# A layer norm, a state-space scan and a gated feed-forward layer on one core: four equal chunks in a hand-planned order, B and C transposed by DMA

## The chip, the cores and the metric

The kernel runs on 1 core of one Trainium2 chip. The metric is the device time of one execution in microseconds (us), lower is better. A kernel is timed several times, in turns with the kernel before on the same chip. Each run carries the span of the core and the mean clock that TensorE was granted. A run counts as "slow" when it is over 1.5% above the fastest run of its kernel; only fast runs enter ratios. The profile's "span" leaves out some 2 us that the timed figure includes.

Engines are named as in the profile: PE is TensorE (matmul), DVE is VectorE, ACT is ScalarE, POOL is GpSimd, SP is SyncE, which here only issues DMAs. Each engine works through its own queue of instructions in order.

## The reference, cut to what matters

Sequence 2048, model width 448, feed-forward width 1792, all bf16.

```python
xn = layernorm(x)                                   # over 448, no scale or bias
# A: diagonal complex state-space layer, 448 states
Lam_bar = exp(dt * Lam);  B_bar = ((Lam_bar - 1) / Lam)[:, None] * B
h[t] = Lam_bar * h[t-1] + B_bar @ xn[t]             # complex, 2048 steps
s = 2 * real(C @ h) + xn * Dskip
# B: gated feed-forward
g = silu((sigmoid(xn @ w_gate) * (xn @ w_up)) @ w_down)
out = x + s * g
```

Both kernels work in chunks of tokens. For a chunk, PE multiplies the transposed normalised input (`xnT`) with gate and up weights (14 "units" `gu`, each one gate and one up tile) and with B (4 units `bu`); ACT evacuates these; DVE rotates, scans and rotates back (the complex recurrence as two real scans) and forms the gated product `hF`; PE then does the down product and the y product (skip term plus C times h) for each 128-token tile.

## The kernel before

Chunks of 256, 512, 512, 512 and 256 tokens. The statistics of the layer norm are taken on DVE, but what turns a variance into 1/sqrt(var) runs for all but the first chunk on GpSimd as Newton steps on tiny tiles. All but the first two chunks' `xn` are transposed by DMA, whose source must be padded with a 64-column copy on GpSimd.

```python
CHUNKS = [(0, 2), (2, 4), (6, 4), (10, 4), (14, 2)]     # first tile, tiles of 128 tokens
N_PE_TR = 2                                             # chunks whose x is transposed on PE

def stat_chain(g):
    G = nc.vector if g == 0 else nc.gpsimd
    ...
    for _ in range(3):                                  # Newton steps for 1/sqrt
        G.tensor_tensor(out=t, in0=y, in1=y, op=ALU.mult)
        G.tensor_tensor(out=t, in0=t, in1=ve, op=ALU.mult)
        G.tensor_scalar(out=t, in0=t, scalar1=-0.5, scalar2=1.5, op0=ALU.mult, op1=ALU.add)
        G.tensor_tensor(out=y, in0=t, in1=y, op=ALU.mult)
    ...
def norm(c, i):                                         # from the third chunk on
    nc.scalar.activation(xm[:], x_all[:, tt, :], ACT.Identity, bias=nmean[:, tt, :])
    nc.scalar.activation(xn[:, i, 0:448], xm[:], ACT.Copy, scale=rsd[:, tt, :])
    nc.gpsimd.tensor_copy(out=xn[:, i, 448:512], in_=xn[:, i, 384:448])
def b_steps():                                          # B (and likewise C): load, then transpose on PE
    ...
    for m in range(7):
        nc.tensor.transpose(tp[:, m, :], b_t[:, m, kt * P:(kt + 1) * P], ident[:, :])
def gu_unit(c, xnT, ft, half_first):
    if c == 0:                                          # tanh form, in the first chunk only
        nc.scalar.activation(th[:], gu[:, 0, 0:n], ACT.Tanh, scale=0.5)
        ...
```

## Time and profile before

Median 242.36 us (241.81 to 245.34).

| engine | busy, us | share of the 238.9 us span |
|---|---|---|
| PE | 204.5 | 86% |
| DVE | 179.4 | 75% |
| ACT | 127.4 | 53% |
| POOL | 36.3 | 15% |

These lines are from the profile's page of the kernel before. The rows with digits cut the span into 40 equal slices; a digit is the busy share of a slice in tenths, and PEclk the granted TensorE clock in tenths of full speed.

```profile
span 238.9 us, 3346 instructions
...
PE 204.5 (86%) x1146; PEld 98.1 (41%) x1160; DVE 179.4 (75%) x444; ACT 127.4 (53%) x254; POOL 36.3 (15%) x102
...
PE   7589538697974999989739999999999999999990
...
DVE  7999179998799999999995792799666369533204
...
PEclk9889955999998999999959999999999999999997
```

Shares over the whole span hide that the limit moves. Counted from 0, PE is poorly used in slices 4 to 7 and has two deep dents at 12 and 20; DVE is full in the middle; after slice 20 PE is full and DVE is not. These are the two costliest of PE's waits (columns: what waited, for what, us in total, times, longest):

```profile
PE bu L425 <- DMA xnT<-xn: 10.1, 2, 5.7
PE tpx L226 <- DVE xn L211: 8.9, 6, 4.9
```

Of DVE's waits, this one:

```profile
DVE xn L211 <- POOL rsd L201: 6.4, 1, 6.4
```

Two stretches in the windows view (stretch, its length, then busy us and instructions of PE, PE weight load, DVE, ACT and POOL, then granted clock, DMA share, GB/s):

```profile
80.00:120.00 40.00, 36.62 (x181) 15.21 (x184) 39.37 (x80) 26.67 (x48) 16.61 (x30) 1.00 0.07 16
124.00:228.50 104.50, 103.72 (x585) 50.67 (x591) 64.70 (x146) 51.32 (x106) 0.50 (x2) 0.99 0.05 16
```

PE stood still twice, 4.5 and 5.7 us, for a transposed x. DVE waited 6.4 us for `rsd` (one over the standard deviation of each token), which GpSimd makes, and PE's transposes waited for DVE in turn. The trace shows why it was late: GpSimd had begun this chain at 13.71 us, then stood 8.9 us before a copy for C whose DMA had not landed, with the rest of the chain behind that copy; it ended at 31.33. Its two later chains, with nothing foreign in them, took 10.7 and 16.2 us. Between 80 and 120 us DVE was busy 39.4 of 40 us, and after 124 us PE 103.7 of 104.5.

### The profile page before, as it was taken

The numbers are of one execution on the slowest core, as the hardware profiler recorded it, in microseconds if no ns is written. First come the engines' busy times: TensorE is split into PE (matmuls) and PEld (weight loads), VectorE is DVE, ScalarE is ACT, GpSimd is POOL, SyncE is SP. The second block draws the span as 40 slices with busy tenths as digits, with TensorE's granted clock in tenths as the row PEclk, the third lists the DMA queues.
The fourth block names the chain that finished last, engine by engine and source line by source line (L and its number), as shares of the span: only waits on it lengthen the run. The fifth ranks groups of instructions, "written<-read, shape, count | busy, mean of one in ns | idle before, by whom it ended". The sixth has DMA issues, their size and how long they took to land.

```text
span 238.9 us, 3346 instructions
## 1 busy us (share of the span) xinstructions
PE 204.5 (86%) x1146; PEld 98.1 (41%) x1160; DVE 179.4 (75%) x444; ACT 127.4 (53%) x254; POOL 36.3 (15%) x102
## 2 busy tenths in 40 slices
PE   7589538697974999989739999999999999999990
PEld 2246316343431444433314444344444455555550
DVE  7999179998799999999995792799666369533204
ACT  3468713478891736676703563874546273533232
POOL 2010720482000068830000000000000000000000
PEclk9889955999998999999959999999999999999997
DMA  6999900000211000011110000020000000000001
GB/s 133 351 277 272 348 27 0 4 0 0 44 23 25 0 19 0 0 44 22 22 41 0 25 0 19 0 65 1 19 19 3 19 0 19 22 21 21 22 0 40
DMA packets 15608, 11.75 MB, mean 49 GB/s; under 512 B 6083, under 2 KB 14662, under 8 KB 15590
## 3 DMA queue, kind: packets, MB, share of 16 engines
q1 hardware_dynamic: 15536, 11.41, 17.2%
q0 software_dynamic: 48, 0.11, 0.4%
q8 instruction: 9, 0.15, 0.3%
q14 instruction: 9, 0.07, 0.1%
q10 hardware_dynamic: 6, 0.00, 0.0%
HBM read 8.37 MB, written 1.84 MB: 43 GB/s over the span
## 4 chain that ended last, share of the span: by engine, by line
PE 48%; DVE 28%; DMA 10%; ACT 5%; POOL 3%; issue 3%; SPq 2%; DVEq 0%; POOLq 0%
PE gu L419 16%; PE acc L586 14%; PE acc L594 6%; DVE wv L517 6%; DMA wk<-in_B_w_gate_dram 5%; PE bu L419 5%; PE gu L425 3%; DMA bc<-in_A_C_im_dram 3%; DMA xnT<-xn 2%; DVE z L510 2%; DVE ta L506 2%; DVE hF L456 2%; DVE tb L508 1%; DVE hT L536 1%; DVE td L534 1%
## 5 line engine op out<-in xcount | busy, mean ns | idle before, releaser
L451 ACT ACTIVATE sig<-gu 128x512 bf16<-128x512 f32 (+1 forms) x56 | 30.4, 543 | 44.8 <-PE gu L425 34.5
L419 PE MATMUL gu<-xnT,wg 128*128 128x512 bf16 (+1 forms) x201 | 47.0, 340 | 2.9 <-ACT ub L455 1.2
L419 PE MATMUL gu<-xnT,wu 128*128 128x512 bf16 (+1 forms) x207 | 48.1, 340 | 0.2
L586 PE MATMUL acc<-wd,hF 128*128 128x448 bf16 x224 | 47.4, 357 | 0.9 <-DVE hF L456 0.8
L456 DVE TENSOR_TENSOR hF<-sig,ub 128x512 bf16<-128x512 bf16 (+1 forms) x56 | 21.0, 385 | 22.9 <-ACT ub L455 22.6
L586 PEld LDWEIGHTS <-hF 128*128 128x128 bf16 x224 | 22.3, 99 | 22.8 <-issue 2.0
L455 ACT CAST ub<-gu 128x512 bf16<-128x512 f32 (+1 forms) x56 | 29.6, 528 | 0.0
L419 PEld LDWEIGHTS <-wu 128*128 128x128 bf16 x210 | 20.8, 99 | 16.4 <-DMA wu<-in_B_w_up_dram 0.2
L419 PEld LDWEIGHTS <-wg 128*128 128x128 bf16 x210 | 17.6, 98 | 23.6 <-issue 12.9
L419 PE MATMUL bu<-xnT,bT 128*128 128x512 bf16 (+1 forms) x103 | 23.9, 367 | 0.7 <-ACT bus_606 L476 0.7
L425 PE MATMUL gu<-xnT,wk 64*128 64x512 bf16 (+1 forms) x140 | 21.2, 343 | 1.3 <-DMA wk<-in_B_w_up_dram 0.6
L594 PE MATMUL acc<-cT,hT 128*128 128x448 bf16 x98 | 20.8, 352 | 0.0
L600 ACT ACTIVATE sigd<-acc 128x448 bf16<-128x448 f32 x16 | 8.7, 544 | 16.1 <-PE acc L586 16.1
L425 PE MATMUL bu<-xnT,bT 64*128 64x512 bf16 (+1 forms) x35 | 7.1, 350 | 11.5 <-DMA xnT<-xn 10.1
L419 PEld LDWEIGHTS <-bT 128*128 128x128 bf16 x105 | 9.8, 104 | 13.0 <-issue 7.1
L594 PEld LDWEIGHTS <-hT 128*128 128x128 bf16 x112 | 11.0, 98 | 10.1
L216 POOL COPY xn<-xn 128x64 bf16<-128x64 bf16 x10 | 4.3, 426 | 70.8 <-ACT xn L215 70.8
L604 DVE TENSOR_TENSOR g_t<-zb,sigd 128x448 bf16<-128x448 bf16 x16 | 6.1, 384 | 11.4 <-ACT zb L602 11.4
L425 PEld LDWEIGHTS <-wk 64*128 64x128 bf16 x140 | 5.2, 94 | 14.3 <-issue 12.6
L226 PE MATMUL tpx<-ident,xn 128*128 128x128 bf16 x24 | 3.3, 279 | 8.9 <-DVE xn L211 8.9
L610 DVE TENSOR_TENSOR sg<-acc,g_t 128x448 bf16<-128x448 f32 x14 | 8.6, 618 | 2.6 <-PE acc L594 2.4
L170 DVE BATCH_NORM_STATS2 stats<-x_all 128x6 f32<-128x448 bf16 x16 | 9.7, 608 | 0.0
(269 smaller groups left out, 299.2 us busy)
## 6 DMA issues: line engine op xcount, KB each, us to landing
out_dram<-o_t SPq DMA_DIRECT2D x16, 112.0 KB, 1.7
wd<-in_B_w_down_dram SPq DMA_DIRECT2D x1, 1568.0 KB, 9.3
x_all<-in_A_x_dram SPq DMA_DIRECT2D x3, 448.0 KB, 7.8
wg<-in_B_w_gate_dram SPq DMA_DIRECT2D x1, 960.0 KB
wu<-in_B_w_up_dram SPq DMA_DIRECT2D x1, 960.0 KB, 11.1
wg<-in_B_w_gate_dram SPq DMA_DIRECT2D x1, 384.0 KB, 5.5
wu<-in_B_w_up_dram SPq DMA_DIRECT2D x1, 384.0 KB, 6.4
bc<-in_A_B_re_dram SPq DMA_DIRECT2D x1, 336.0 KB, 10.7
```

The costliest lines, as they stand in the source:

```text
L170: nc.vector.bn_stats(out=stats[:], in_=x_all[:, t0 + i, :])
L419: nc.tensor.matmul(banks[i][:, 0:n], lhsT=fulls[i](kt), rhs=xnT[:, kt, 0:n], start=(kt == 0 and not half_first), stop=(kt == KF - 1 and ha ...
L425: nc.tensor.matmul(banks[i][:, 0:n], lhsT=halves[i], rhs=xnT[lo:lo + H, 3, 0:n], start=half_first, stop=not half_first)
L451: sg_ins = nc.scalar.activation(sig[:, 0:n], gu[:, 0, 0:n], ACT.Sigmoid).ins
L455: nc.scalar.copy(out=ub[:, 0:n], in_=gu[:, 1, 0:n])
L456: anchors["hF"] = nc.vector.tensor_tensor(out=hF, in0=sig[:, 0:n], in1=ub[:, 0:n], op=ALU.mult).ins
L517: V.tensor_tensor_scan(out=cell["wv"][:, k, 0:n], data0=rb, data1=cell["z"][:, k, 0:n], initial=(st[pt][:, k, :] if c else 0.0), op0=ALU.m ...
L586: nc.tensor.matmul(dacc[:, 0:D], lhsT=hFs[c][:, ft, j * P:(j + 1) * P], rhs=wd[:, ft, :], start=(ft == 0), stop=(ft == FT - 1))
L594: nc.tensor.matmul(y[:, 0:D], lhsT=hTs[c][:, hm, j * P:(j + 1) * P], rhs=K["cT"][:, cm, :], start=False, stop=(i == 6))
L600: nc.scalar.activation(sigd[:], dacc[:, 0:D], ACT.Sigmoid, scale=half)
L604: nc.vector.tensor_tensor(out=g_t[:], in0=zb[:], in1=sigd[:], op=ALU.mult)
L610: nc.vector.tensor_tensor(out=sg[:], in0=y[:, 0:D], in1=g_t[:], op=ALU.mult)
```

## The change

The intent is to keep PE full throughout: equal 512-token chunks, an order of every engine's instructions laid down by a small planner with estimated durations ("late" work that is ready at a time, "side" work that fills DVE's gaps), B and C brought in already transposed by DMA so that PE and ACT are rid of 60 block transposes, and the tanh form of the gate for the larger first chunk. The diff is 1322 lines; its core, with cuts marked:

```diff
-CHUNKS = [(0, 2), (2, 4), (6, 4), (10, 4), (14, 2)]
-N_PE_TR = 2
+CT = 4                       # tiles in a chunk; NCH = 4 chunks
+N_TANH = FT + 2              # gates in the tanh form
 ...
-    nc.sync.dma_start(out=b_t[:, 0:3, 0:448], in_=A_B_re[0:384, :].rearrange("(i p) d -> p i d", p=P))
 ...
+    def load_b():
+        for k, mat in enumerate((A_B_re, A_B_im)):
+            nc.sync.dma_start_transpose(out=bT[:, 0:3, a:a + 384], in_=mat[0:384, 0:384])
+            if k == 0:
+                nc.sync.dma_start_transpose(out=bw[:], in_=mat[0:384, 320:448])
 ...
+    load_w(512, 1152)
+    load_b()
+    load_w(1152, F)
 ...
+    T_CHAIN = 9.0            # the planner's estimate of GpSimd's statistics chain
+    def stat_chain(g, t0, n):            # 19 GpSimd instructions, 26 before; 3 Newton steps as before
+        plan.add_late(plan.dve + T_CHAIN, 0.15, fin)      # fin: rsd = 1/sd_b, on DVE
 ...
+    def norm_slot(tt, on_vector):
+        xm = norm_a(tt, False)                            # ACT
+        plan.force(lambda: tt // CT in rs_done)
+        norm_b(tt, xm, False)                             # ACT, needs rsd
+        dup(tt)                                           # GpSimd: 64-column copy
+        dma_transpose(tt)
 ...
+    def b_fix():
+        nc.gpsimd.tensor_copy(out=bT[LO, 3, 0:384], in_=bw[HI, 0, :])
+    run_phase(G(0, 2, 8) + mixed(G(0, 8, 14), Bs(0), 2), [], spread(norms(1, True), 4, 5) + [(3, b_fix)])
+    ssm(0)                   # puts the scan of chunk 0, C's scaling and the statistics of chunk 3 into DVE's side list
+    ssm(1)
+    u = mixed(G(1, 0, 4), []) + mixed(G(1, 4, 8), Bs(1)) + G(1, 8, 14)
+    run_phase(u, spread(downs(0), 1, 8), spread(norms(2), 2, 8))
 ...
```

## The prediction

> **What bounds the kernel now.** The page gives PE 86%, DVE 75%, ACT 53% busy of a 238.9 us span; the limit moves. The chain of waits and the timeline show:
> - Head: the first gate/up matmul starts at 10.85 us.
> - 10.8 to 46.5 us: only the 256-token chunk 0. PE is busy 15.0 us of 10.8 to 30 and 5.2 of 30 to 40; it waits for x statistics (DVE waits 6.4 us for GpSimd), then transposes x tiles and 28 B blocks.
> - 40 to 120 us: DVE is busy 39.4 of 40 us from 80 to 120. PE stalls twice for the transposed x (4.46 and 5.66 us), and resumes at granted clock 0.62 and 0.50.
> - 124 to 228.5 us: PE-bound, 103.7 of 104.5 us busy, DVE only 64.7.
>
> **PE work that remains.** From starts in the timeline: a pair of gate/up units takes 3.23 us (153.31 to 156.54), a down tile 2.65, a y tile 1.52. My sum per 512-token chunk: 14 units 22.6 + B units 5.7 + four downs 10.6 + four y 6.1 = 45 us; four chunks 180 us. The 28 B and 32 C block transposes on PE, about 8 us with waits, go to DMA.
>
> **DVE work.** At the starts in the chain (0.60 us a 1024-wide multiply, 1.20 a scan), a chunk's scan part is 23 us; all DVE work is about 175 us, unchanged: the float32 tanh gate product now covers 16 x 512 columns. The 256-wide one took 0.42, so I estimate 0.65: +4.5 us. DVE and PE are nearly balanced, so the order must overlap them throughout.
>
> **Sum.** Statistics of four tiles precede the first norm, so the first gate/up matmul slips to about 12; two units in halves make it worth a full-rate start near 14. 14 + 180 + 4 (last product, add, store) = 198 us. Losses I add: 2 us in chunk 0, where ACT has 14 x 1.05 + sines 5.5 + B copies 4.3 = 24 us against about 25 of PE; 2 us spread (DVE has about 43 us of work against 39 of PE in the chunk-1 phase). Span 202; the wall time was 2 to 3.5 over the span before. **Predicted 205 us, 198 to 217** (8 in 10); faster by 2%: 0.97, within 0.02, slower 0.01.
>
> **DMA.** B's DRAM transposes stand before the last third of the gate/up weights on one queue. One 128x512 on-chip transpose took 1.19 us to issue, 2.4 to land. Scaled by 128x128 blocks, B's eight issues are about 10 us: weights land near 25, needed near 28. The Trainium skill, "DMA: Bandwidth & Descriptors", section "Latency and other measured facts", gives 261 GB/s for DMA transposes: 3.5 us for B's 0.92 MB, an estimate. The trace before has none from DRAM.
>
> **What would show it.** PE busy above 88%; no PE gap over 2 us after the first unit; PE-bound last three chunks; B and C transposes landing before first use; the x transposes never on PE's wait list.
>
> **What would make it wrong.** (1) DRAM transposes much slower to issue: PE waits for the last weights or bT at 28 to 35 us. (2) The GpSimd copy of the last tile of chunk 2 stands behind the statistics chain for chunk 3; a late DVE starves PE there. (3) A stall above 3 us costs more afterwards: the Trainium skill, "TensorE: Matmul & The Clock Gate", section "HAM oscillation", says idle gaps over about 3.4 us halve the clock; this trace agrees, clock 0.50 after the 5.66 us gap.

## The result, and the profile after

Median 223.56 us of four runs (220.67 to 225.65); two of the four were slow, and so was the profiled one. The ratio to the kernel before is 0.911 (95% interval 0.898 to 0.925): faster by 9%, where 205 us would have been 15%. A ratio is the mean time of one kernel's fast runs over that of the other's fast runs of the same rounds, so it is not quite the ratio of the medians quoted. Time and ratio lie above the predicted range.

The changed kernel was run again unaltered.

> The changed kernel again, unedited, as the control of this set: 220 to 222 us in its fast runs.

Measured: median 222.06 us, mean of its fast runs 221.7, ratio 0.915 (0.906 to 0.924), profile fast. It is the control below: "the changed kernel" means this profile unless said otherwise. Its page:

```profile
span 219.2 us, 2849 instructions
...
PE 195.6 (89%) x978; PEld 82.4 (38%) x978; DVE 178.0 (81%) x379; ACT 121.3 (55%) x218; POOL 34.0 (15%) x88
...
PE   7789976979993899929999999999999999959992
...
DVE  5756982946994299996589999999999999999943
...
PEclk9999999999999699966999999999999999999999
```

Against before, the second half is as planned: PE slices of 9 almost to the end. What is left of the weak stretch are three dents, in slices 6, 12 and 17, the last two with a lower clock after them. PE's waits name them:

```profile
PE bu L476 <- ACT bus L548: 5.4, 2, 4.3
PE gu L470 <- DMA xnT<-xn: 4.4, 1, 4.4
PE bu L476 <- POOL bT L831: 2.9, 1, 2.9
PE acc L678 <- DVE g_t L686: 2.3, 2, 1.2
```

Here `bu` is PE's product with B and `bus` ACT's copy of it, which frees PE's output memory for the next one; `bT` is the transposed B; `g_t` is DVE's gated output, which frees the memory of the y product (`acc`).

The three longest waits are 2.88, 4.29 and 4.43 us, 11.6 together, and have three different names behind the arrow: a GpSimd copy, an ACT copy, a DMA. The timeline of PE shows where they lie (start, length, engine, line, operation, and in brackets the idle time before it):

```profile
34.95 0.39 PE L476 MATMUL bu<-xnT,bT 64*128 64x512 bf16 x2 [2.88 <-POOL bT L831]
...
71.94 0.61 PE L476 MATMUL bu<-xnT,bT 64*128 64x512 bf16 x2 [4.29 <-ACT bus L548]
...
97.44 1.46 PE L470 MATMUL gu<-xnT,wg 128*128 128x512 bf16 x3 [4.43 <-DMA xnT<-xn]
```

Now GpSimd's timeline in the same execution, with the starts and ends of three runs of its statistics chain (19 small instructions each):

```profile
24.63 0.68 POOL L241 CAST var_b<-mv 128x4 bf16<-128x4 f32 x1 [13.47 <-DVE mv L226]
...
33.68 0.65 POOL L260 TENSOR_TENSOR sd_b<-y,ve 128x4 bf16<-128x4 f32 x1
34.40 0.50 POOL L831 COPY bT<-bw 64x384 bf16<-64x384 bf16 x1
...
58.69 0.95 POOL L241 CAST var_b<-mv 128x4 bf16<-128x4 f32 x1 [15.88 <-DVE mv L226]
...
64.30 0.99 POOL L256 TENSOR_TENSOR q<-y 128x4 f32<-128x4 f32 x1
...
66.02 0.98 POOL L258 TENSOR_SCALAR q<-q 128x4 f32<-128x4 f32 x1
...
67.72 0.20 POOL L256 TENSOR_TENSOR q<-y 128x4 f32<-128x4 f32 x1
...
68.84 0.20 POOL L260 TENSOR_TENSOR sd_b<-y,ve 128x4 bf16<-128x4 f32 x1
...
84.87 0.56 POOL L241 CAST var_b<-mv 128x4 bf16<-128x4 f32 x1 [2.69 <-DVE mv L226]
...
94.42 0.34 POOL L260 TENSOR_TENSOR sd_b<-y,ve 128x4 bf16<-128x4 f32 x1
94.71 0.23 POOL L293 COPY xn<-xn 128x64 bf16<-128x64 bf16 x1
```

- First stall: the copy that finishes B's transpose (`bT`, 34.40) stands behind the chain of chunk 1, which runs from 24.63 to 34.33. PE starts at 34.95. The copy takes 0.50 us, and its data was there long before: that transpose was issued at 12.48 and landed 4.3 us later.
- Third stall: the 64-column copy of chunk 2's last tile (94.71) stands behind the chain of chunk 3, from 84.87 to 94.76. The DMA transpose is issued at 94.97 and PE starts at 97.44.
- Second stall: the chain of chunk 2 ends at 69.04. DVE then makes `rsd`; ACT, whose queue has the norm of chunk 2 ahead of a copy that PE needs, waits for it. ACT's timeline:

```profile
69.35 0.67 ACT L289 ACTIVATE xn<-xm,rsd 128x448 bf16<-128x448 bf16 x1 [5.35 <-DVE rsd L263]
...
70.87 1.02 ACT L548 CAST bus<-bu 128x1024 bf16<-128x1024 f32 x1
```

ACT stood still 5.35 us before `xn`, although the copy `bus` behind it needed nothing from the norm. PE got its bank of memory back after 71.9.

Why does a chain of 19 instructions on 128x4 elements take 10 us? From 67.72 on, with DVE idle, its instructions take 0.20 us each. Before that they take up to 0.99. The next fence is DVE's timeline beside them:

```profile
64.09 1.22 DVE L584 TENSOR_TENSOR_SCAN wv<-r_col,z 128x512 bf16<-128x512 f32 x1
...
65.80 1.21 DVE L584 TENSOR_TENSOR_SCAN wv<-r_col,z 128x512 bf16<-128x512 f32 x1
...
69.07 0.18 DVE L263 RECIPROCAL rsd<-sd_b 128x4 f32<-128x4 bf16 x1 [1.49 <-POOL sd_b L260]
```

The GpSimd instruction that began at 64.30 ended at 65.29; the DVE scan beside it ran from 64.09 to 65.31. The one from 66.02 ended at 67.00, the scan at 67.01. GpSimd waited for DVE's instruction to end. The Trainium skill, "SBUF — State Buffer", section "Who interferes with whom", says this: a DVE instruction with two SBUF inputs and a GpSimd instruction that reads SBUF share one read interface, and the one that comes second is blocked for the whole instruction. This trace agrees. So the chain is slow because DVE is busy: at 0.28 us from start to start, as from 67.72 on, 19 instructions would take about 5.3 us (an estimate), and the other half is waiting. Experiment 3 shows the same chain in 5.6 us, started where DVE has little to do.

A word on the clock. The Trainium skill, "TensorE: Matmul & The Clock Gate", section "HAM oscillation", puts the limit of an idle gap at about 3.4 us. In this profile the gap of 2.88 us left the clock at full, those of 4.29 and 4.43 us were followed by 0.50. In the first, slow profile the same first gap was 3.58 us long and half clock followed it. Over all profiles, after the first 10 us, the limit is not so sharp. Every PE gap of 3.58 us or more was followed by half clock, and none of 1.2 to 1.46 us was; between them both happened. A gap of 2.14 us was followed by 0.50 in experiment 4 and by full clock in experiment 7, one of 3.10 us by 0.50 in experiment 9 and one of 3.16 us by full clock in experiment 8. So whether half clock follows a gap of 1.6 to 3.2 us can't be read from its length. That may be why this kernel's runs scatter; it was not tested by itself.

### The profile page after: what moved, and what is told of

The parts are those of the page before. It is cut to its first block, busy times and chain, and to the rows that moved or that the text cites. A ratio compares the mean times of both kernels' runs of the same rounds, so it can differ in the third digit from the quotient of the medians.

```text
span 223.9 us, 2849 instructions
## 1 busy us (share of the span) xinstructions
PE 199.6 (89%) x978; PEld 83.6 (37%) x978; DVE 178.2 (80%) x379; ACT 121.5 (54%) x218; POOL 33.4 (15%) x88
## 4 chain that ended last, share of the span: by engine, by line
DVE 51%; PE 22%; POOL 12%; ACT 8%; issue 4%; DMA 1%; POOLq 0%; ACTq 0%
DVE wv L584 9%; PE gu L470 8%; PE acc L665 5%; DVE stats L225 3%; DVE hT L604 3%; PE acc L680 3%; DVE g_t L686 3%; DVE tb L565 2%; DVE ta L565 2%; DVE hFa L526 2%; DVE z L578 2%; DVE hFb L526 2%; PE bu L470 2%; DVE x_all L687 2%; PE wps L214 2%
## 5 line engine op out<-in xcount | busy, mean ns | idle before, releaser
L519 ACT ACTIVATE sig<-gu 128x512 bf16<-128x512 f32 x40 | 23.9, 597 | 30.2 <-PE gu L476 22.8
L665 PE MATMUL acc<-wd,hFb 128*128 128x448 bf16 x112 | 23.8, 353 | 0.0
L665 PE MATMUL acc<-wd,hFa 128*128 128x448 bf16 x112 | 23.8, 353 | 0.0
L520 ACT CAST ub<-gu 128x512 bf16<-128x512 f32 x40 | 23.2, 581 | 0.0
L470 PE MATMUL bu<-xnT,bT 128*128 128x512 bf16 x84 | 23.1, 412 | 0.0
L515 ACT ACTIVATE th<-gu 128x512 f32<-128x512 f32 x16 | 9.5, 596 | 12.6 <-PE gu L476 9.5
L665 PEld LDWEIGHTS <-hFa 128*128 128x128 bf16 x112 | 11.0, 98 | 10.7
L665 PEld LDWEIGHTS <-hFb 128*128 128x128 bf16 x112 | 11.0, 98 | 10.2
L526 DVE TENSOR_TENSOR hFa<-sig,ub 128x512 bf16<-128x512 bf16 x19 | 7.9, 417 | 7.2 <-ACT ub L520 7.1
L686 DVE TENSOR_TENSOR g_t<-acc,g_t 128x448 bf16<-128x448 f32 x16 | 9.9, 618 | 1.9 <-PE acc L680 1.8
```

The source lines that it names most:

```text
L470: nc.tensor.matmul(banks[i][:, cols], lhsT=fulls[i](kt), rhs=xnT[:, kt, cols], start=(kt == 0 and not half_first), stop=(kt == KF - 1 and ...
L515: nc.scalar.activation(th[:], gu[:, 0, :], ACT.Tanh, scale=0.5)
L519: nc.scalar.activation(th[:], gu[:, 0, :], ACT.Sigmoid)
L520: nc.scalar.copy(out=ub[:], in_=gu[:, 1, :])
L526: V.tensor_tensor(out=hF, in0=th[:], in1=ub[:], op=ALU.mult)
L665: nc.tensor.matmul(dacc[:, 0:D], lhsT=hF_at(c, ft)[:, j * P:(j + 1) * P], rhs=wd[:, ft, :], start=(ft == 0), stop=(ft == FT - 1))
```

## The experiments

Gains are given as differences of ratios times the 242 us of the kernel before, because the runs had different chips. Theory Q: the missing 17 us are PE and DVE waiting for results that stand behind the statistics chain in GpSimd's queue. Its rivals: the DRAM transposes deliver B late; a late DVE is the real limit, so that reorders on GpSimd give almost nothing; and (T, tried last) the chain costs time by itself, whatever stands behind it. Three kinds of test tell them apart: move what stands behind the chain (1 to 4), change only its length (5 to 7), and relieve or load DVE (8 to 10).

**1. B's copy first.** The copy now stands ahead of the chain in GpSimd's queue; it ran at 16.23 us.

```diff
+    nc.gpsimd.tensor_copy(out=bT[LO, 3, 0:384], in_=bw[HI, 0, :])     # right after a dummy Silu
 ...
-    run_phase(..., spread(norms(1, True), 4, 5) + [(3, b_fix)])
+    run_phase(..., spread(norms(1, True), 4, 5))
```

> The copy of the last rows of B into bT (0.50 us on GpSimd) is put ahead of the statistics chain of chunk 1 in GpSimd's order. Theory Q (GpSimd's queue): PE's 3.58 us wait for this copy goes, the half clock after it too, and DVE's 5.88 us idle at 35 us; bw landed long before, so the copy runs near 18 us; time falls by about 6 us against the changed kernel's fast 221.4. Rival R (the DRAM transposes are late): the wait stays and is ended by a transfer into bT or bw; time within 1 us. Rival D (DVE's total work alone sets the end): the wait goes but time falls by under 2 us.

Measured 217.92 us, ratio 0.9031 (0.8977 to 0.9085). The wait for `bT` is gone from PE's list and nothing else came in its place; the other two stalls stay:

```profile
PE bu L476 <- ACT bus L548: 5.4, 2, 4.3
PE gu L470 <- DMA xnT<-xn: 4.4, 1, 4.4
```

The gain by ratios is 2.9 us, half of what was expected. The expectation was sized from the slow profile, where the gap was 3.58 us and half clock followed; in the fast control it was 2.88 with no half clock. Since PE no longer waits for `bT` at all, the data was there: the rival of late DRAM transposes falls.

**2. The 64-column copy on ACT.** It then no longer stands behind the chain of chunk 3.

```diff
-        dup(tt)
+        nc.scalar.activation(xns[tt // CT][:, tt % CT, 448:512], xm[:, 384:448], ACT.Copy, scale=rsd[:, tt, :])
```

> The 64-column copies of chunks 2 and 3 go from GpSimd to ACT, so the last one no longer stands behind the statistics chain of chunk 3. All theories: PE's 4.42 us wait for xnT at 97 to 101.7 us goes. Rival P (each PE stall costs itself and the half clock after it): time falls by about 6 us. Theory Q with DVE behind: DVE was busy through this stall but for 1.90 us, so PE only reaches the first y tile earlier and waits there for DVE; time falls by 1 to 3 us.

Measured 218.71 us, ratio 0.9044 (0.8989 to 0.9098), 2.6 us by ratios. PE's wait for the DMA of `xnT` is gone. The stall and the half clock after it were worth 4.43 and some 2.3 us; less came back, within the 1 to 3 us that theory Q expected with DVE close behind. DVE is nearly full after the stall: 87.6 of 90 us from 110 to 200 us in the control (PE 87.7). That PE then waits for DVE instead is likely but not shown by this run, whose only profile is a slow one.

**3. Chunk 2's statistics earlier.** They move ahead of the sign flips and coefficients in DVE's list, so that the chain starts sooner (at 48.85 us, as it turned out, where it was 58.69).

```diff
     side.append((0.0, emit_edges))
+    for i in range(4):
+        side.append((0.7, lambda i=i: stat(2, 8, i, 4)))
+    side.append((0.0, lambda: stat_chain(2, 8, 4)))
     side.append((0.9, emit_neg))
     side.append((2.2, emit_coeffs))
-    for i in range(4):
-        side.append((0.7, lambda i=i: stat(2, 8, i, 4)))
-    side.append((0.0, lambda: stat_chain(2, 8, 4)))
```

> The statistics of chunk 2 are taken before the sign flips and coefficients, in DVE's idle stretch at 50.6 to 55.2 us, so their GpSimd chain starts about 10 us earlier. Theory Q: ACT's 5.36 us wait for the reciprocal goes, with it PE's 4.29 us wait for bus and about 7 us of DVE idle at 72 to 80 us; time falls by about 6 us. Rival D: the order of the same DVE work changes nothing; within 2 us.

Measured 218.6 us, ratio 0.9042 (0.8983 to 0.9102), 2.7 us by ratios. The longest PE wait for ACT's `bus` fell from 4.29 to 1.1 us. Again about half of what was expected. GpSimd's chain, first and last instruction:

```profile
48.85 0.29 POOL L241 CAST var_b<-mv 128x4 bf16<-128x4 f32 x1 [5.93 <-DVE mv L226]
...
54.26 0.20 POOL L260 TENSOR_TENSOR sd_b<-y,ve 128x4 bf16<-128x4 f32 x1
```

The same 19 instructions took 5.6 us here and 10.35 in the control; DVE was busy 3.6 us of them here, mostly with instructions of 0.16 us, and 8.9 there. So part of the gain can come from the shorter chain and not from its place. ACT is now the busy one of the stretch: DVE's wait for `ctmp`, which ACT makes for C, rose from 3.8 us in one piece to 5.3 in four.

**4. All three together.**

> All three edits. Theory Q: the DVE idle that goes is about 5.9 + 7 + 1.9 = 15 us, so about 206 to 208 us, near the 205 predicted, with DVE over 90% busy from 20 us to the end and no PE wait over 2 us before the tail. Rival P: the three PE stalls with their half-clock stretches, about 19 us, go: 202 us. Rival D: 217 us or more.

Measured 210.81 us, ratio 0.8731 (0.8687 to 0.8776), 10.2 us by ratios. The three single gains sum to 8.2 us; their intervals are 1.3 to 1.5 us either way and the control's is 2.1, so whether they add is not settled. The time is 2.8 us above the 206 to 208 expected, and one PE wait over 2 us is left before the tail. PE's longest waits in this kernel:

```profile
PE acc L678 <- DVE g_t L686: 3.3, 3, 2.1
PE bu L476 <- ACT bus L548: 2.5, 2, 1.4
```

And stretches of its windows view:

```profile
100.00:140.00 40.00, 38.65 (x196) 16.32 (x194) 39.26 (x76) 25.65 (x49) 0.00 (x0) 1.00 0.09 22
140.00:180.00 40.00, 40.00 (x205) 17.48 (x204) 39.23 (x72) 19.64 (x37) 0.00 (x0) 1.00 0.04 12
181.00:183.00 2.00, 0.03 (x1) 0.03 (x1) 1.93 (x6) 0.00 (x0) 0.00 (x0) 1.00 0.00 0
183.00:187.00 4.00, 3.69 (x12) 1.40 (x12) 3.85 (x8) 0.00 (x0) 0.00 (x0) 0.57 0.08 29
```

No wait names GpSimd or a DMA any more, except GpSimd's at the start of the warm-up. PE is busy 40.0 of 40 us from 140 on, and DVE over 39 of 40 from 100 on: both are full there. At 181 us PE waits 2.14 us for DVE's `g_t`, and the clock falls to 0.57 on average over the next 4 us, 0.50 between 184 and 187.

**5 and 6. The length of the chain alone.** No reorder; only the number of Newton steps changes, 3 to 1 and 3 to 6. (One step was still accurate enough for the comparison with the reference.)

```diff
-        for _ in range(3):
+        for _ in range(1):        # and 6 in the other run
```

> One Newton step in place of three in the three GpSimd chains (8 of 19 instructions, about 4.1 us, less in each; the result moves by less than bfloat16 rounding); every order stays. Theory Q: the bT copy runs near 31.6 us, before PE needs it at 32.7; ACT's wait for the reciprocal falls from 5.4 to about 1 us; the copy of the last tile of chunk 2 comes 4 us earlier; all three PE waits shrink below 1.5 us and time falls by 8 to 11 us, close to the three reorderings together. Rival R (late transposes) and rival D (DVE's total): within 2 us, as no transfer and no DVE work changes.

> Six Newton steps in place of three: 12 more GpSimd instructions, about 6.2 us more per chain. Theory Q: all three PE waits grow by about 6 us each, to 9 to 11 us; time rises by 15 to 19 us, to about 237 to 240. Rival R and rival D: within 2 us.

Measured: one step 213.44 us, ratio 0.8795 (0.8712 to 0.8879), a gain of 8.6 us; six steps 234.81 us, ratio 0.9697 (0.9622 to 0.9772), a loss of 13.2. With one step (a slow profile) the wait for `bT` is gone and that for the DMA of `xnT` is 1.0 us, but the longest for `bus` is still 2.7, over the 1.5 expected. PE's waits with six steps:

```profile
PE bu L476 <- ACT bus L548: 8.8, 2, 7.6
PE gu L470 <- DMA xnT<-xn: 7.7, 1, 7.7
PE bu L476 <- POOL bT L831: 6.0, 1, 6.0
```

All three stalls grew by about the same amount: 2.88 to 6.0, 4.29 to 7.6, 4.43 to 7.7, about 3.2 us each. They share a cause, and it is the chain; a rule that names the releaser gave three names for it. Twelve more instructions were expected to cost over 6 us; they cost some 3.3, because by then DVE had itself run out of work and blocked nothing: in chunk 2's chain the last 16 of the Newton instructions took 0.20 us each, 0.28 from start to start, and 12 times 0.28 is 3.4. The loss of 13.2 is a little under the expected 15 to 19 for the same reason.

**7. The chain shortened and the three reorders together.** If the reorders had only hidden part of the chain's cost, shortening it would still pay.

> The three reorders (210.8 us, ratio 0.873) and the shortened statistics chain together (1 Newton step in place of 3; the shortened chain alone gave 213.0 us, ratio 0.8795). Theory Q (the loss is PE and VectorE waiting for results that stand behind the chain in GpSimd's queue; the reorders have taken away those waits already): the shorter chain finds nearly nothing left, 208.5 to 211.5 us, ratio 0.86 to 0.875. Rival T (the chain also costs time that the reorders don't touch, by sharing VectorE's memory path or by making coefficients late): gains add at least in half, 204 to 207 us, ratio 0.845 to 0.857.

Measured 211.9 us, ratio 0.8748 (0.869 to 0.8806): the same as the three reorders alone, although GpSimd's busy time fell from 26.7 to 18.7 us. Once nothing that PE or ACT needs stands behind it, the chain costs nothing that these runs can tell: the difference is 0.4 us the other way, with intervals of 1.1 and 1.4 us either way. T expected a ratio of 0.857 or less and falls.

**8. The residual add moved to GpSimd**, on top of the three reorders, for all but the last chunk: the obvious way to relieve DVE.

```diff
-            V.tensor_tensor(out=x_all[:, tt, :], in0=g_t[:], in1=x_all[:, tt, :], op=ALU.add)
+            (V if c == NCH - 1 else nc.gpsimd).tensor_tensor(out=x_all[:, tt, :], in0=g_t[:], in1=x_all[:, tt, :], op=ALU.add)
```

> The three edits together, and the last add of the 12 tiles of chunks 0 to 2 goes from DVE to the now idle GpSimd (12 x 0.31 = 3.7 us off DVE). Theory D2 (with the GpSimd waits gone, DVE sets the time of the second half): 3 to 4 us less than the three edits alone (210.8), PE's 2.14 us wait for DVE at 183 us gone. Rival (PE is then the limit): within 1 us. Rival (GpSimd's two-input add slows DVE instructions beside it): no gain, with longer DVE instructions.

Measured 213.41 us, ratio 0.881 (0.8713 to 0.8907): no gain (1.9 us worse by ratios, with intervals that overlap). Two of GpSimd's adds:

```profile
146.26 1.94 POOL L687 TENSOR_TENSOR x_all<-g_t,x_all 128x448 bf16<-128x448 bf16 x1 [28.54 <-DVE g_t L686]
...
156.25 1.03 POOL L687 TENSOR_TENSOR x_all<-g_t,x_all 128x448 bf16<-128x448 bf16 x1 [3.76 <-DVE tq L637]
```

DVE's work beside the first:

```profile
146.09 1.27 DVE L584 TENSOR_TENSOR_SCAN wv<-r_col,st,z 128x512 bf16<-128x512 f32 x1
147.41 0.81 DVE L592 TENSOR_TENSOR tq<-wv,sinL 128x2 f32<-128x2 bf16 x1
```

And beside the other:

```profile
156.27 1.02 DVE L638 SCALAR_TENSOR_TENSOR st<-wv,cosL,tq 128x1 f32<-128x1 bf16 x1
```

The add begun at 146.26 came during a scan that ended at 147.36, and took 1.94 us; one that had the interface to itself took 1.03 (DVE does it in 0.39). DVE's two-element `tq`, 0.15 us elsewhere, began at 147.41 and ended at 148.22, with the add's end at 148.20. `st`, 0.22 us elsewhere, took 1.02 and ended with the add at 157.28. The same lock as in the chain, seen from DVE's side. DVE was spared 12 instructions of 0.39 us, yet its busy time rose from 177.9 to 180.3 us, and PE's wait for `g_t` from 3.3 to 5.5.

**9. More work for DVE.** Is DVE or PE the limit after the reorders? Twelve useless 128x448 additions on DVE, 0.385 us each, tell.

> The three edits, and 12 useless DVE adds of 128x448 (12 x 0.31 = 3.7 us), one after the store of each tile of chunks 0 to 2; the outputs don't change. Theory D2 (DVE sets the pace of the second half once the GpSimd waits are gone): 3 to 4 us more than the 210.8 of the three edits, 214 to 215. Rival (PE sets it): less than 1 us more.

The output was wrong (not a number), and PE waited 5.8 us for a transposed x before the first addition even ran. The time, 220.25 us, means nothing.

> Repeats the failed extra-VectorE-work run without its new tile: 12 extra 128x448 bf16 additions on VectorE (about 0.39 us each, 4.7 us in all) in the first three chunks, written over the tile of the warm-up matmuls, on top of the three reorders (210.8 us). The output should be correct. If VectorE's queue is the limit of the middle chunks (it was 97 per cent busy there): +3.5 to +5.5 us, 214 to 216. If PE is the limit there: 0 to +1.5 us, 210.8 to 212.3.

Wrong again, 221.12 us. The order of SP's instructions showed the slip: the added lines were indented one level too little, so the store behind them left the deferred function. Twelve stores of the output were issued from 38.0 to 44.9 us, before their data existed, ahead of the transposes of x in the same queue; the last chunk's were never issued. The edit as it should have been:

```diff
             V.tensor_tensor(out=x_all[:, tt, :], in0=g_t[:], in1=x_all[:, tt, :], op=ALU.add)
+            if c < NCH - 1:
+                V.tensor_tensor(out=warm[:, 0:448], in0=g_t[:], in1=g_t[:], op=ALU.add)
             nc.sync.dma_start(out=out_flat[tt * P:(tt + 1) * P, :], in_=x_all[:, tt, :])
```

> The two earlier forms of this run were wrong through a slip of the edit, found in the order of the instructions: the lines put into the deferred function were indented one level too little, so that the stores of the output left the function and went out before their data was there, ahead of the transposes in the same queue. Here the 12 extra additions of 128x448 on VectorE (some 0.39 us each, 4.7 us in all) stand inside the function. The output should be correct. If VectorE's queue is the limit of the middle chunks: +3.5 to +5.5 us over the three reorders' 210.8, 214 to 216. If PE is the limit there: 0 to +1.5 us, 210.8 to 212.3.

Correct, 213.85 us, ratio 0.8842 (0.8805 to 0.8878). For 4.6 us of added DVE work (12 at 0.385) the time rose 2.7 us by ratios, 3.0 by medians: over half of it, between the two expected bands. PE's waits show it arriving:

```profile
PE acc L678 <- DVE g_t L686: 4.6, 3, 3.1
...
PE acc L665 <- DVE g_t L686: 1.8, 2, 1.0
```

`g_t` waits rose from 3.8 to 6.4 us in sum (from 3.3 and 0.5 to 4.6 and 1.8). So DVE's queue does limit the end of the middle part, with little slack, and PE is close behind.

**10. The skip term on PE.** The product `xn * Dskip` (1.08 us of DVE a chunk) goes: PE multiplies `xnT` with a diagonal matrix instead of adding a prepared tile. The edit also makes that matrix once on DVE and keeps four `xnT` buffers and two `xm` where it had two and three (both not shown).

```diff
-        nc.tensor.matmul(y[:, 0:D], lhsT=ident[:, :], rhs=xnds[c][:, j, :], start=True, stop=False)
+        for kt in range(4):
+            r, n = (ALL_P, P) if kt < 3 else (LO, H)
+            nc.tensor.matmul(y[:, kt * P:kt * P + n], lhsT=xnTs[c][r, kt, j * P:(j + 1) * P],
+                             rhs=diag[r, kt * P:kt * P + n], start=(kt == 0), stop=False)
```

> The three edits, and the four DVE products with Dskip (1.0 us each) are gone: PE multiplies the transposed x by a diagonal of Dskip, four matmuls of at most 128 columns (estimate 0.22 us) in place of one of 448 (0.19 us) per tile. Theory D2: 3 to 4 us less than 210.8, about 207. Rival (PE sets it): 0 to 1 us more.

Measured 210.13 us, ratio 0.8687 (0.8641 to 0.8734): 1.1 us better than the three reorders by ratios, with intervals that overlap. The 2.14 us wait is gone and PE is busy 20.00 of 20 us from 180 to 200, where it was not before. DVE's busy time fell 3.3 us, but PE's rose 1.3, and the expected 3 to 4 us did not come. That PE is now the limit of the end is likely but not shown: the chain of work that ended last is 82% PE in this profile (28% in the three reorders'), but 58% DVE in that of experiment 13, which has the same diagonal term.

**11. More room for ACT's work on C.** On the three reorders, two scan steps of DVE for each step of C instead of one (`k = 2` in the planner), to spread ACT's `ctmp`.

```diff
-            k = 1
+            k = 2
```

> The three edits, and the seven scalings of C come after every second scan step of chunk 0 instead of every step. In the three-edit run ACT is busy 9.91 us of 60 to 70 and DVE idles 5.7 us in 53 to 68 waiting for its scaled C. Theory A2 (ACT is the limit there and the idle is paid for at the end): DVE's idle for it falls below 2 us and time by 2 to 4 us. Rival (that idle is slack): within 1 us.

Measured 211.71 us, ratio 0.876 (0.8731 to 0.8789): no gain. DVE's wait for `ctmp` stayed (6.1 us against 5.7). The edit also puts off the statistics of chunk 3, so this rules out the edit, not the cause.

**12 and 13. A combination, and what spoiled it.** The three reorders, the diagonal skip term, two Newton steps and `k = 2`; then the same without `k = 2`.

> All: the three edits, the diagonal, the spread of C, and two Newton steps in place of three. If the two theories hold and add up: 203 to 206 us, faster than every kernel so far. If the idle and DVE gains overlap: 207 to 209.

> The three reorders and the diagonal skip term (209.8 us, ratio 0.8687), with 2 Newton steps in place of 3 and without the other edit of the combined version (two side items per tile, ratio 0.8837). If the two side items per tile were what made the combined version slower: 208 to 210 us, ratio 0.861 to 0.870. If the shorter chain upset the planned order: 212 to 214 us, ratio 0.878 to 0.886.

Measured 213.61 us, ratio 0.8837 (0.8804 to 0.887), where 203 to 209 us were expected, and without `k = 2` 210.42 us, ratio 0.8664 (0.8615 to 0.8714). So two Newton steps cost nothing, and `k = 2`, worth 0.7 us against it in experiment 11, cost some 4 together with the diagonal term. With it PE was busy 8.57 us and DVE 7.88 from 100 to 110 us, without it 9.95 and 9.79; why is open. The best versions, those of 10 and 13, are at 210 us not to be told apart: 13% below the kernel before, and 11 to 12 us below the change as it was given.

## Why the prediction was wrong

**Sign and mechanism: right.** Faster by over 2% was given 0.97. PE's pieces came as read from the trace before: a pair of units 3.23 us, a down tile 2.65, a y tile 1.52. From 105 to 215 us PE was busy 107.7 of 110 us. PE was busy 89% of the span, above the 88% claimed.

**The sum of needed work, 198 us: right to about 1 us.** An estimate from the control's profile: the waits of PE on its list after the first units (bus 5.4, xnT by DMA 4.4, bT 2.9, g_t 2.3, ub 0.6, wk 0.5) are 16.1 us. The half clock afterwards cost 4 us x (1 - 0.64) + 5 us x (1 - 0.53) = 3.8, from the granted clock of the windows 71.9 to 75.9 and 97.4 to 102.4. The span of 219.2 less these 19.9 is 199.3. The same sum for the three reorders (7.7 and 1.7 us from 208.6) gives 199.2.

**The step that failed: "Losses I add: 2 us in chunk 0 ... 2 us spread."** Four us of losses measured 19.9, and those 15.9 are nearly the whole miss of 17.2 (a span of 219.2 against 202). The reorders took away 10.5 of them (19.9 to 9.4), which is roughly what hung on GpSimd's chain; the other 5.4 are taken up under "2 us spread" below. With it fell "no PE gap over 2 us after the first unit" (three, of 2.88, 4.29 and 4.43 us) and "the x transposes never on PE's wait list" (4.4 us).

- Risk (2), the copy behind the chain of chunk 3, was named in so many words, and it happened: 4.43 us and about 2.3 of half clock. It was priced at nothing in the sum and hardly in the range.
- Two other routes from the same chain were not seen: the `bT` copy behind chunk 1's chain, and ACT standing before chunk 2's `rsd` with PE's copy behind it. Both could have been read from the order of instructions. The profile before showed what the chain takes, 10.7 and 16.2 us for its 26 instructions, and the planner's own figure for it is 9.0.
- That it was this chain is shown twice over: taking away what stood behind it gave back 10.2 us, shortening it without any reorder 8.6, doing both no more than the first, and lengthening it made each stall longer by about the same 3.2 us.

**Risk (1), slow DRAM transposes: wrong cause, though they were slower than estimated.** B's eight issues held SP from 10.5 to 22.1 us, 11.6 us against an estimate of 10, and the last weights delayed PE by 0.5 us. B's data was never late once its copy had its place.

**Risk (3), a stall costs more afterwards: right.** 3.8 us in the fast control. In the first, slow profile the gap of 3.58 us alone was followed by 6.7 us at a mean clock of 0.54, which is 3.1 us more (an estimate).

**"2 us spread", DVE behind: half right.** DVE's busy time was 178.0 us against about 175. After the reorders it is full from 100 us on, and 4.6 us more of it cost 2.7. Of the 9.4 us of losses that the three reorders still have, the waits for DVE's `g_t` are 3.8, the half clock after one of them 1.7 and ACT's `bus` 2.5; the prediction had allowed 4 in all. "PE-bound last three chunks" held only in part: PE was busy 107.7 of 110 us there, but the chain of work that ended last is 52% DVE and 21% PE in the control.

## What to carry to other kernels

When an order is planned by hand, plan the slow helper engine too: list for its in-order queue what stands behind each long run of small instructions, and who waits for that. Three waits with three names (a copy, an ACT bank, a DMA) were one chain; lengthening the suspect and seeing all of them grow by the same amount showed it more cheaply than three repairs. A named risk belongs in the sum, with its size times its chance, not only in the list of what may go wrong.

## What the Trainium skill lacked or had wrong

- "SBUF — State Buffer", section "Who interferes with whom": the lock between GpSimd and two-input DVE instructions is stated there and these runs agree (GpSimd adds 1.03 us alone, 1.94 when begun during a scan; DVE's `tq` 0.15 us alone, 0.81 beside an add). What it lacks is what this does to many tiny instructions: 128x4 elements took 0.20 us each with DVE idle and up to 1.11 beside scans, so that a chain of 19 took 9.7 to 10.4 us, and 5.6 where DVE had little to do.
- "TensorE: Matmul & The Clock Gate", section "HAM oscillation": about 3.4 us as the limit held for four gaps of the changed kernel (2.88 us: full clock; 3.58, 4.29 and 4.43: half). In the three reorders a gap of 2.14 us was followed by clock 0.50 from 184 to 187 us, and a gap of 2.14 us in experiment 7 by full clock; the shortest gap with half clock after it was 1.61 us (one Newton step, a slow profile; 1.92 in a fast one, experiment 12). So a gap well under the limit is not safe.
- "DMA: Bandwidth & Descriptors", section "Latency and other measured facts": 261 GB/s for DMA transposes (given there for a non-contiguous middle dimension) is no guide for transposes from DRAM issued one after another. B's 0.92 MB took 11.6 us to issue in eight pieces of 1.23 to 1.89 us, about 79 GB/s, and the first of C held the queue for 6.35 us. For the time that such an issue holds its queue this section has no figure; elsewhere the page has only cycle counts of earlier generations, for small tiles and for one large on-chip transpose.
